# A chunked-attention and gated-FFN kernel whose order of work comes from another model of transfers and of two engines

## The chip, the cores and the metric

The kernel runs on one core of a Trainium2 chip. TensorE (PE) multiplies matrices, VectorE (DVE), ScalarE (ACT) and GpSimd (POOL) do elementwise work, and SyncE (SP) issues every transfer (DMA). Each engine runs its own instructions strictly in the order in which they stand in the program, and waits on semaphores for the others. The metric is the device time of one execution in microseconds (us), less being better. Three runs of the kernel before took 854.36, 854.88 and 857.61 us; the median is 854.88 us.

## What is computed

Inputs are float32: q, k, v of 8 batches x 8 heads x 576 positions x 64, w_in (512 x 2048) and w_out (2048 x 512).

```python
q_c, k_c, v_c = [a.reshape(B, H, 9, 64, D) for a in (q, k, v)]      # chunks of 64
scores = np.matmul(q_c, k_c.transpose(0, 1, 2, 4, 3)) / np.sqrt(D)
attn = np.exp(scores - scores.max(-1, keepdims=True))
attn = attn / (attn.sum(-1, keepdims=True) + 1e-09)
x = np.matmul(attn, v_c).reshape(B, H, S, D).transpose(0, 2, 1, 3).reshape(B * S, H * D)
h = x @ w_in                                                        # 4608 x 2048
g = h * (1.0 / (1.0 + np.exp(-1.702 * h)))
out = (g @ w_out).astype(np.float32)                                # 4608 x 512
```

## The kernel before

**Tiling.** The 4608 tokens are 36 tiles u of 128 and 9 blocks n of 512 (NB = 9, BT = 512); d_ff is 16 tiles j of 128 (NF = 16). A pair number g = 16 n + j names one block and one tile of d_ff. A float32 product is made of three matmuls: each operand is split into a high and a low part (`h`, `l`), and `w_h x_l + w_h x_h + w_l x_h` is summed in PSUM.

**Stages.** Blocks 0 and 1 use the plain product: steps h0_g and h_g, 12 matmuls of 128x512 (L1205 to L1207). Block 2 (g = 32 to 47) uses seven products instead of eight on halves, the scheme of Strassen and Winograd: for each pair p of tiles j there are seven products P1 to P7 of six matmuls of 128x256, in four phases ph0 to ph3 (`plan_seven`, L684 to L686). Blocks 3 to 8 go two at a time, s = 0, 1, 2, with the same seven products of six matmuls of 128x512 (`plan_two`, L770 to L772). After every product GELU and the split of g follow (steps gh_g on ACT, gl_g on DVE: L817, L721, L1232), and the second matmul, four steps o_g_0 to o_g_3 of three matmuls each (L1242 to L1244), into four PSUM banks po0 to po3 that hold a block's output until ob_n_t copies it (ACT for even t, DVE for odd) and st_n_t stores it. The copies go through two buffers, `ob`.

**Weights of the seven products.** `plan_prep` makes, for each p, sums of w_in's quarters on POOL (`sums`), splits them (phi on ACT, plo on DVE, L588), and writes all seven to a DRAM tensor `seven`: the three quarters that are no sums by out_a (steps pout0 to pout2, L595), the sums by out_s (pouts, L600). Block 2 loads them by phase (ld0 to ld3, L674, into a ring of six slots, 512 floats a product), blocks 3 to 8 by product (L763, six pieces).

**x's sums.** The seven products need sums of x as well. `plan_x(r, h, ..)` makes four differences t1 to t4 of 128x512 (L511, on POOL) for r = 0 (block 2) and, for each run of two blocks r = 1, 2, 3, for two halves h; ACT takes the high parts (L524) and DVE the low parts (L527).

**Attention** runs beside this, two tiles at a time (u = 4, 6, .. 34). From u = 6 on, q and k arrive as many small transfers (qk_i_n_u, L924 or L913, into one buffer `raw`), are transposed on DVE (tq0_u, tq1_u, L967), and step s_u on PE makes the scores of u (L983) and, in the same step, x of the pair before (L1057), which needs the transposed exponentials et_(u-2) of DVE (L1032), the load v1_(u-2) and both PSUM buffers `hp`. Between the two stand max and difference (mx, m), exp, sum (z) and POOL's normalisation n_u (L1013). v has one buffer, which s_(u+2) gives back.

**What sets the order.** `Plan` is a list scheduler that runs while the program is built. Every step is added with an engine, a cost in us written by hand, a rank, the events that it needs, and the buffers that it takes and gives. `emit` plays this list on model engines: whenever an engine is free, it takes the ready step of lowest rank. The order that comes out is the program's order on each engine; nothing of it is decided on the chip. ORDER fixes the first steps by name. In this model a small transfer keeps the DMA engine for its cost and lands 2.9 us later; a large one (`bulk`) issues in 0.5 us and then keeps a bus (BUS) for its cost. POOL and DVE know nothing of each other.

In the lists of order below a row is one instruction or several equal ones; the name ahead of `<-` is what is written, its last number only counts allocations.

Of the kernel before, what the change touches and what calls it, by code (L numbers as in the profile page):

```python
# [9 lines left out]
F32 = mybir.dt.float32  # L10
# [4 lines left out]
AF = mybir.ActivationFunctionType  # L15
ALU = mybir.AluOpType
AX = mybir.AxisListType

PE, ACT, DVE, POOL, DMA, BUS = "pe", "act", "dve", "pool", "dma", "bus"
# [28 lines left out]
class Plan:  # L48
# [6 lines left out]
    HANDOVER = {None: 0.0, PE: 0.25, ACT: 0.12, DVE: 0.12, POOL: 0.15, DMA: 2.9, BUS: 2.4}  # L55
    TABLE_LOAD = 1.3

    def __init__(self, buffers):
        self.free = dict(buffers)
        self.steps = []  # L60
        self.first = {}

    def add(self, engine, cost, rank, fn, need=(), make=None, take=(), give=(), table=None):
        self.steps.append((engine, cost, rank, fn, tuple(need), make, tuple(take), tuple(give), table))

    def bulk(self, cost, rank, fn, need=(), make=None, take=(), give=()):

        self.add(DMA, 0.5, rank, fn, need=need, make=make + "~", take=take)
        self.add(BUS, cost, rank, None, need=[make + "~"], make=make, give=give)

    def emit(self):
# [12 lines left out]
        busy = {e: 0.0 for e in self.HANDOVER}  # L84
        first = {e: names.split()[::-1] for e, names in self.first.items()}
# [3 lines left out]
        while left:  # L89
            for e, heap in ready.items():  # L90
                while heap and busy[e] <= now + 1e-9:
# [13 lines left out]
                    _, cost, _, fn, _, make, take, give, tab = self.steps[pick]  # L105
# [7 lines left out]
                    left -= 1  # L113
                    busy[e] = now + cost
                    post(now + cost, 0, () if e in (DMA, BUS) else give)
                    post(now + cost + self.HANDOVER[e], 0, give if e in (DMA, BUS) else ())
                    post(now + cost, 1, (make, e, True))
                    post(now + cost + self.HANDOVER[e], 1, (make, e, False))
            assert at or not left, sorted((s[2], s[5]) for h in ready.values() for s in [self.steps[i] for _, i in h])[:9]
            now = at[0][0] if at else now  # L120
            while at and at[0][0] <= now + 1e-9:
# [4 lines left out]
                else:  # L126
                    ev, engine, same = what
                    for i in users.get(ev, ()):
                        to = self.steps[i][0]
                        if (to == BUS or (to == engine and engine != DMA)) != same:  # L130
                            continue
# [10 lines left out]
def tile_chunk_attention_ffn(  # L142
# [29 lines left out]
    RANKS = (2.5, 8.5, 14.0, 16.5, 26.5, 29.5, 34.5, 39.0, 46.0, 53.5, 59.0, 72.0, 73.5, 78.5, 84.5, 101.5)  # L172
    K_ACT = (1, 2, 3, 4)
    LEAD = 12
# [31 lines left out]
    X_SLOT = (9, 10, 11, 12, 6, 4, 2, 3, 15, 5, 13, 14, 7, 8)  # L206
# [19 lines left out]
    def plan_w(j):  # L226
# [48 lines left out]
        plan.add(DMA, 2.85, rank - 5.5, load, need=need, make=e("raw"), take=[f"w{j}"])  # L275
# [1099 lines left out]
```

## Time and profile before

| what | value |
| --- | --- |
| median of three runs | 854.88 us |
| the profiled execution, its own time | 857.12 us |
| its span, first to last instruction | 855.3 us |
| granted TensorE clock, mean | 0.991 |
| PE busy | 821.2 us, 96% of the span |
| DVE / ACT / POOL busy | 550.1 / 378.0 / 125.2 us |
| DMA packets, bytes | 235303, 128.95 MB |

A busy PE is the bound, so what counts is where PE stood idle and at which clock it ran. A row of the view of waits reads: engine, what it was about to write, its line, then what ended the wait, and us in total, times, longest. A row of a timeline reads: start, length, engine, line, what is written from what, how many, and in brackets the idle time before it with what ended it. A row of the view by stretches reads: the stretch, its length, busy us of PE, PE's weight load, DVE, ACT, POOL (with counts), the granted clock of PE, the share in which the DMA engines were busy, and GB/s.

### The profile page before, as it was taken

What the parts mean: (1) busy time and instruction counts of PE and PEld (TensorE: products, weight loads), DVE (VectorE), ACT (ScalarE), POOL (GpSimd) and SP (SyncE); (2) the same over time, 40 slices, a digit from 0 to 9 for tenths busy, and PEclk for the clock granted to TensorE, in tenths of its full rate; (3) what the DMA queues carried; (4) which work ended last, traced back from release to release, by engine and by line L of the source; (5) the groups of instructions that cost most, each with busy time, mean ns of one, the idle gap of its engine ahead of it and who ended that gap; (6) DMA issues with size and microseconds to landing.
All of it is one profiled execution on the core that took longest, in us unless ns stands there. A gap on an engine that the chain in (4) does not pass through costs nothing.

```text
span 855.3 us, 15198 instructions
## 1 busy us (share of the span) xinstructions
PE 821.2 (96%) x5894; PEld 680.0 (80%) x5894; DVE 550.1 (64%) x741; ACT 378.0 (44%) x557; POOL 125.2 (15%) x102
## 2 busy tenths in 40 slices
PE   7999997999998999999999999999999999999998
PEld 6888876888887887888887778888877788888786
DVE  5778966656965789757768877593468443443322
ACT  5989724526615246343436344342444222323222
POOL 1000343474100113000002310000022000000000
PEclk9999998999998999999999999999999999999999
DMA  9996765676469876765576446644441054444101
GB/s 231 326 310 185 205 185 161 173 221 182 90 212 248 222 186 140 192 160 136 146 176 163 74 102 154 164 132 118 133 124 38 1 154 120 122 123 124 49 1 50
DMA packets 235303, 128.95 MB, mean 151 GB/s; under 512 B 186592, under 2 KB 200928, under 8 KB 235232
## 3 DMA queue, kind: packets, MB, share of 16 engines
q1 hardware_dynamic: 235232, 127.98, 56.3%
q8 instruction: 47, 0.77, 0.4%
q14 instruction: 24, 0.20, 0.1%
HBM read 103.81 MB, written 24.12 MB: 150 GB/s over the span
## 4 chain that ended last, share of the span: by engine, by line
PE 68%; SPq 10%; DVE 9%; DMA 8%; ACT 3%; issue 2%; POOL 1%; DVEq 0%; POOLq 0%; ACTq 0%
PE po L1242 11%; PE po L1243 11%; PE po L1244 11%; PE hp L770 8%; PE hp L772 8%; PE hp L771 8%; SPq L924 5%; DMA raw<-in_moe_w_out_dram 3%; PE x L1057 2%; DMA w<-seven 2%; PE s L983 2%; DVE w L527 1%; DVE g_l L817 1%; DVE eT L1032 1%; PE hp L1205 1%
## 5 line engine op out<-in xcount | busy, mean ns | idle before, releaser
L1242 PE MATMUL po<-w,g_l 128*128 128x512 f32 x576 | 228.8, 397 | 8.3 <-DVE g_l L817 5.9
L1243 PE MATMUL po<-w,g_h 128*128 128x512 f32 x576 | 225.1, 391 | 0.0
L1244 PE MATMUL po<-w,g_h 128*128 128x512 f32 x576 | 224.7, 390 | 0.0
L1242 PEld LDWEIGHTS po<-w,g_l 128*128 128x128 f32 x576 | 108.5, 188 | 35.8 <-DVE g_l L817 10.0
L1244 PEld LDWEIGHTS po<-w,g_h 128*128 128x128 f32 x576 | 108.4, 188 | 23.0
L1243 PEld LDWEIGHTS po<-w,g_h 128*128 128x128 f32 x576 | 108.6, 189 | 20.9
L808 ACT ACTIVATE g<-g 128x512 f32<-128x512 f32 x48 | 30.2, 632 | 143.1 <-DVE g L759 142.9
L770 PE MATMUL hp<-w,w 128*128 128x512 f32 x224 | 87.5, 391 | 2.2 <-DVE w L527 1.6
L772 PE MATMUL hp<-w,w 128*128 128x512 f32 x224 | 87.2, 389 | 0.0
L771 PE MATMUL hp<-w,w 128*128 128x512 f32 x224 | 87.2, 389 | 0.0
L1032 DVE STREAM_TRANSPOSE eT<-e 32x512 f32<-32x512 f32 x120 | 84.2, 702 | 1.9
L1013 POOL TENSOR_TENSOR e<-e,r 128x1024 f32<-128x1024 f32 x16 | 32.3, 2017 | 326.0 <-DVE r L1010 240.0
L817 DVE TENSOR_TENSOR g_l<-g,g_h 128x512 fp32r<-128x512 f32 x48 | 39.5, 822 | 53.9 <-ACT g_h L813 53.7
L813 ACT ACTIVATE g_h<-g 128x512 fp32r<-128x512 f32 x48 | 30.3, 630 | 74.5 <-PE po L1244 72.5
L967 DVE STREAM_TRANSPOSE qkT<-raw 128x1024 f32<-128x1024 f32 x30 | 37.0, 1238 | 25.8 <-DMA raw<-in_k_dram 15.0
L1205 PE MATMUL hp<-x_l,w 128*128 128x512 f32 x120 | 48.1, 401 | 5.1 <-DVE g_l L1232 5.1
L770 PEld LDWEIGHTS hp<-w,w 128*128 128x128 f32 x224 | 42.0, 188 | 12.4 <-DVE w L527 1.5
L772 PEld LDWEIGHTS hp<-w,w 128*128 128x128 f32 x224 | 42.0, 188 | 8.7
L771 PEld LDWEIGHTS hp<-w,w 128*128 128x128 f32 x224 | 42.1, 188 | 8.6
L1207 PE MATMUL hp<-x_h,w 128*128 128x512 f32 x120 | 47.6, 396 | 1.3 <-DVE w L266 1.3
L1206 PE MATMUL hp<-x_h,w 128*128 128x512 f32 x120 | 47.7, 397 | 0.0
L759 DVE TENSOR_TENSOR g<-hp,g 128x512 f32<-128x512 f32 x24 | 16.6, 691 | 43.6 <-PE hp L772 43.3
(140 smaller groups left out, 1385.9 us busy)
## 6 DMA issues: line engine op xcount, KB each, us to landing
w<-seven SPq DMA_DIRECT2D x120, 256.0 KB, 2.8
pieces<-seven SPq DMA_DIRECT2D x56, 256.0 KB, 2.9
w<-seven SPq DMA_DIRECT2D x24, 512.0 KB, 4.5
raw<-in_moe_w_in_dram SPq DMA_DIRECT2D x16, 512.0 KB, 7.6
raw<-in_moe_w_out_dram SPq DMA_DIRECT2D x16, 512.0 KB, 7.9
out_dram<-ob SPq DMA_DIRECT2D x32, 256.0 KB, 2.2
seven<-w SPq DMA_DIRECT2D x16, 512.0 KB, 3.8
raw<-in_q_dram SPq DMA_DIRECT2D x208, 32.0 KB, 2.6
```

The costliest lines, as they stand in the source:

```text
L770: nc.tensor.matmul(hp, w[:, 0, c], xl[:, c], start=c == 0, stop=False)
L771: nc.tensor.matmul(hp, w[:, 0, c], xh[:, c], start=False, stop=False)
L772: nc.tensor.matmul(hp, w[:, 1, c], xh[:, c], start=False, stop=c == 1)
L817: nc.vector.tensor_tensor(gl, words(h, late), gh.bitcast(F32), op=ALU.subtract)
L924: nc.sync.dma_start(t[p0 : p0 + 32, i, n, o // 32 : (o + c) // 32, :], src[b, 2 * n + h, s : s + c, d * 32 : d * 32 + 32].rearrange("(t j) ...
L1032: nc.vector.transpose(st["et"][po : po + 32, :, 32 * a : 32 * a + 32], st["e"][pi : pi + 32, :, 32 * b : 32 * b + 32],)
L1205: nc.tensor.matmul(hp, wh, xl, start=cc == 0, stop=False)
L1206: nc.tensor.matmul(hp, wh, xh, start=False, stop=False)
L1207: nc.tensor.matmul(hp, wl, xh, start=False, stop=cc == NCC - 1)
L1242: nc.tensor.matmul(po, gl[:, c], w[:, 0, :], start=first, stop=False)
L1243: nc.tensor.matmul(po, gh[:, c], w[:, 0, :], start=False, stop=False)
L1244: nc.tensor.matmul(po, gh[:, c], w[:, 1, :], start=False, stop=last)
```

## The change

The model behind the order changes, and with it some work:

- Transfers. BUS is gone. A transfer has a count and a time each; each issues in 0.48 us, not before the transfer eight places ahead of it has landed (LANES = 8), lands no earlier than 2.1 us after its start, and not before the one ahead plus its own time.
- Port. Steps of POOL, and those of DVE marked `port`, are made to wait for each other in the model.
- x's sums of r = 1, 2, 3 are done by DVE (L535 of the changed kernel) instead of POOL: 24 instructions. Those of r = 0 stay on POOL.
- w_in's quarters go to DRAM in two transfers for each p (512 KB and 256 KB) instead of three of 256 KB, with rank `first + 3` instead of `first - 6`; P1 and P2 now lie interleaved in `seven`, and blocks 3 to 8 read them in runs of 1 KB. The sums' rank is `first - 3` instead of `first - 2`.
- Block 2's phases are P1 P2, P6 P7, P5 P3, P4 instead of P1, P2 P6, P5 P3, P7 P4, and their sums are built by seven DVE instructions of 128x256 and one ACT copy for each p, where five DVE instructions (three of 128x256, two of 128x512) and one ACT copy did it.
- LEAD, the ranks of the 16 pairs and some slots are other numbers.

```diff
-    HANDOVER = {None: 0.0, PE: 0.25, ACT: 0.12, DVE: 0.12, POOL: 0.15, DMA: 2.9, BUS: 2.4}
+    HANDOVER = {None: 0.0, PE: 0.25, ACT: 0.12, DVE: 0.12, POOL: 0.15, DMA: 0.1}
+    ISSUE, LANES, LANDING = 0.48, 8, 2.1
...
     def bulk(self, cost, rank, fn, need=(), make=None, take=(), give=()):
-        self.add(DMA, 0.5, rank, fn, need=need, make=make + "~", take=take)
-        self.add(BUS, cost, rank, None, need=[make + "~"], make=make, give=give)
+        self.add(DMA, (1, cost), rank, fn, need=need, make=make, take=take, give=give)
+    def transfers(self, now, count, each):
+        for _ in range(count):
+            start = max(now, self.landed[-self.LANES])
+            now = start + self.ISSUE
+            self.landed.append(max(start + self.LANDING, self.landed[-1] + each))
+        return now, self.landed[-1]
...
+                    if port:
+                        cost += max(0.0, held[POOL if e == DVE else DVE] - now)
+                        held[e] = now + cost
+                    if e == DMA:
+                        free, done = self.transfers(now, *cost)
+                        cost = free - now
+                    else:
+                        done = now + cost
...
-    RANKS = (2.5, 8.5, 14.0, 16.5, 26.5, 29.5, 34.5, 39.0, 46.0, 53.5, 59.0, 72.0, 73.5, 78.5, 84.5, 101.5)
+    RANKS = (-10.5, 9.0, 14.0, 21.0, 26.5, 28.5, 35.0, 39.0, 45.5, 49.5, 61.0, 72.0, 76.5, 85.5, 94.0, 101.5)
-    LEAD = 12
+    LEAD = 27
+    PREP = -3
+    SUMS = 3
+    ON_POOL = (0,)
...
+        T_ENGINE, T_COST, engine = (POOL, 1.05, nc.gpsimd) if r in ON_POOL else (DVE, 0.69, nc.vector)
...
-            nc.gpsimd.tensor_tensor(raw(out), raw(a), raw(b), op=ALU.subtract)
+            engine.tensor_tensor(raw(out), raw(a), raw(b), op=ALU.subtract)
...
-            plan.bulk(0.75, first - 6, lambda i=i: out_a(i), need=[w0 if i < 2 else w1], make=outs[i])
+        for i in range(2):
+            plan.bulk((1.5, 0.85)[i], first - PREP, lambda i=i: out_a(i), need=[(w0, w1)[i]], make=outs[i])
...
-    PHASE = (("P1",), ("P2", "P6"), ("P5", "P3"), ("P7", "P4"))
-    LOADS = ((0, 1), (1, 3), (3, 5), (5, 7))
+    PHASE = (("P1", "P2"), ("P6", "P7"), ("P5", "P3"), ("P4",))
+    LOADS = ((0, 2), (2, 4), (4, 6), (6, 7))
...
-            nc.scalar.activation(st["d"][:, 2:3], st[0][:, :1], AF.Copy)
+            nc.scalar.activation(st["d"][:, 1], st[0][:, 0], AF.Copy)
+        def drain_0b():
+            d = st["d"]
+            add(d[:, 0], st[0][:, 1], d[:, 1])
         def drain_1():
             d = st["d"]
-            add(d[:, 0:2], st[1], bc(d[:, 2:3]))
+            add(d[:, 1], st[1][:, 0], d[:, 1])
+            add(d[:, 2], st[1][:, 1], d[:, 1])
         def drain_2():
             d = st["d"]
-            add(d[:, 2:3], st[2][:, :1], d[:, 1:2])
-            add(d[:, 3:4], st[2][:, 1:], d[:, 2:3])
+            st["f"] = f = more.tile([P, 2, 256], F32, tag="wtmp", name=f"f_{g0}")
+            add(d[:, 3], st[2][:, 0], d[:, 1])
+            add(f[:, 1], st[2][:, 0], d[:, 2])
+            add(d[:, 3], st[2][:, 1], d[:, 3])
         def drain_3():
-            st["f"] = f = more.tile([P, 2, 256], F32, tag="wtmp", name=f"f_{g0}")
-            add(f, bc(st[3][:, :1]), st["d"][:, 1:3])
-            add(f[:, :1], st[3][:, 1:], f[:, :1])
+            add(st["f"][:, 0], st[3][:, 0], st["d"][:, 2])
...
-        plan.add(ACT, 0.42, g0 - 6, drain_0, need=[e("ph0")], make=e("d0"), take=["tmp"], give=["hp"])
+        plan.add(ACT, 0.42, g0 - 6, drain_0, need=[e("ph0")], make=e("d0"), take=["tmp"])
+        plan.add(DVE, 0.42, g0 - 6, drain_0b, need=[e("d0")], make=e("d0b"), give=["hp"])
```

What the new order does to three places, engine by engine.

SP between the loads of pair 8 (`raw_8`) and the first output stores (`ob_0`), before:

```order
L924 DMA raw_8_1103<-in_k_dram 32x8x32 x16
L595 DMA seven_80<-w_8_828 128x2x256 x2
L595 DMA seven_80<-w_9_872 128x2x256
L595 DMA seven_80<-w_10_960 128x2x256 x2
L595 DMA seven_80<-w_11_976 128x2x256
L595 DMA seven_80<-w_12_1064 128x2x256 x2
L595 DMA seven_80<-w_13_1101 128x2x256
L924 DMA raw_10_1322<-in_q_dram 32x8x32 x4
L595 DMA seven_80<-w_14_1173 128x2x256 x2
L595 DMA seven_80<-w_15_1218 128x2x256
L924 DMA raw_10_1322<-in_q_dram 32x8x32 x8
L315 DMA v_8_1455<-in_v_dram 128x8x64
```

The same place in the changed kernel:

```order
L964 DMA raw_8_1069<-in_k_dram 32x8x32 x16
L620 DMA seven_80<-w_12_1028 128x1024
L623 DMA seven_80<-w_13_1118 128x2x256
L620 DMA seven_80<-w_14_1172 128x1024
L623 DMA seven_80<-w_15_1190 128x2x256
L964 DMA raw_10_1339<-in_q_dram 32x8x32 x8
L338 DMA v_8_1442<-in_v_dram 128x8x64
L964 DMA raw_10_1339<-in_q_dram 32x8x32 x4
L1298 DMA out_0_dram<-ob_0_0_1452 128x512
```

The first store of block 0's output (the last row above) is in the order before the row behind those shown; 25 transfers stand between pair 8's last load and it before, 17 now. The stores of w_in's quarters that are gone from here stand further up, the first of them (`w_0`) ahead of 28 loads of pair 6.

DVE in block 2, around the transposes of pair 16 (`qkT_16`) and of pair 14's exponentials (`eT_14`), before:

```order
L721 TENSOR_TENSOR g_l_34_2676<-d_34_2582,g_h_34_2675 128x512
L1032 STREAM_TRANSPOSE eT_14_2605<-e_14_2481 32x16x32 x2
L721 TENSOR_TENSOR g_l_35_2710<-f_34_2683,g_h_35_2709 128x512
L689 TENSOR_TENSOR d_36_2728<-hp_36_1_2715,d_36_2728 128x512
L527 TENSOR_TENSOR w_12_1064<-xs_12_2479,w_11_976 128x2x256
L967 STREAM_TRANSPOSE qkT_16_2506<-raw_16_2223 128x1024
L689 TENSOR_TENSOR d_36_2728<-hp_36_2_2749,d_36_2728 128x256 x2
```

The same place in the changed kernel:

```order
L719 TENSOR_TENSOR f_34_2676<-hp_34_3_2664,d_34_2626 128x256
L1007 STREAM_TRANSPOSE qkT_16_2551<-raw_16_2182 128x1024
L1072 STREAM_TRANSPOSE eT_14_2712<-e_14_2561 32x16x32 x2
L756 TENSOR_TENSOR g_l_34_2692<-d_34_2626,g_h_34_2691 128x512
L1072 STREAM_TRANSPOSE eT_14_2712<-e_14_2561 32x16x32 x6
L756 TENSOR_TENSOR g_l_35_2734<-f_34_2676,g_h_35_2733 128x512
L719 TENSOR_TENSOR d_36_2741<-hp_36_0_2699,d_36_2741 128x256
```

The second transpose of pair 16 now stands ahead of g_l_34 and g_l_35 instead of behind them, and on PE step s_16 stands after o_35_1 instead of after o_36_1, ahead of eight steps that it followed (o_35_2, o_35_3, ph2_36, ph3_36, ph0_38, ph1_38, o_36_0, o_36_1). On SP the load v1_14 that s_16 needs stands 339th instead of 357th among all transfers, and the last load of pair 16 333rd instead of 344th.

DVE at the end of run s = 0, where x's sums of r = 2 are due (`xt_2_0`, `xs_24`), before (POOL holds the four sums):

```order
L991 TENSOR_REDUCE m_26_4949<-s_26_4863 128x16
L1253 COPY ob_3_1_4964<-po_3_1_3795 128x512
L527 TENSOR_TENSOR w_3_540<-xs_24_4942,w_2_524 128x2x256
L527 TENSOR_TENSOR w_5_636<-xt_2_0_4956,w_15_1218 128x2x256
L817 TENSOR_TENSOR g_l_79_4979<-g_0_7_4804,g_h_79_4978 128x512
L527 TENSOR_TENSOR w_4_583<-xs_24_4942,w_6_729 128x2x256
```

The same place in the changed kernel:

```order
L1031 TENSOR_REDUCE m_26_4957<-s_26_4871 128x16
L1293 COPY ob_3_1_4970<-po_3_1_3811 128x512
L535 TENSOR_TENSOR xt_2_0_4975<-xs_24_4950 128x512
L535 TENSOR_TENSOR xs_24_4950<-xs_24_4950,xs_20_4001 128x512
L857 TENSOR_TENSOR g_l_79_4984<-g_0_7_4816,g_h_79_4983 128x512
L535 TENSOR_TENSOR xt_2_0_4975<-xs_24_4950 128x512
L535 TENSOR_TENSOR xs_20_4001<-xs_20_4001,xt_2_0_4975 128x512
```

Two of the sums stand where two low parts stood, and the low parts follow behind g_l_79.

117 lines of the change are left out of this document (64 added, 53 removed).

## The prediction

> **What bounds the kernel now.** I read the page's busy times first, then the view by stretches, then TensorE's waits, then the timelines around each wait.
>
> ```profile
> PE 821.2 (96%) x5894; PEld 680.0 (80%) x5894; DVE 550.1 (64%) x741; ACT 378.0 (44%) x557; POOL 125.2 (15%) x102
> ```
>
> TensorE is busy for 821.2 of 855.3 us, and the change neither adds nor removes a matmul: the same seven products run in another grouping. So the time can fall only by TensorE's 34 us of idle time and by whatever it lost to a lower clock.
>
> ```profile
> 220.00:340.00 120.00, 110.51 (x1095) 97.06 (x1095) 92.37 (x134) 52.60 (x82) 18.57 (x12) 0.97 0.72 190
> 340.00:460.00 120.00, 120.00 (x885) 99.31 (x884) 83.21 (x118) 48.11 (x75) 6.80 (x5) 1.00 0.65 164
> ```
>
> By stretches the idle time is lumpy: 9.5 us in block 2 (220 to 340), none from 340 to 460, although VectorE is busy there for 83 of 120 us.
>
> ```profile
> PE po L1242 <- DVE g_l L817: 5.9, 6, 1.4
> PE hp L1205 <- DVE g_l L1232: 5.1, 2, 4.9
> PE x L1057 <- DMA v<-in_v_dram: 3.7, 1, 3.7
> PE x L419 <- ACT first_b L410: 2.4, 2, 1.3
> PE hp L684 <- issue: 1.8, 1, 1.8
> PE hp L770 <- DVE w L527: 1.6, 2, 1.1
> PE warm L1314 <- POOL ident masks.py:199: 1.4, 1, 1.4
> PE hp L1207 <- DVE w L266: 1.3, 1, 1.3
> PE po L1242 <- DVE g_l L721: 1.3, 1, 1.3
> PE po L1242 <- DVE ob L1253: 1.0, 2, 0.6
> PE s L983 <- DVE qkT L967: 0.9, 1, 0.9
> ```
>
> Leaving out the two of the start (L419, warm), whose steps ORDER still fixes, these are 22.6 us, 17 waits. They are what the new order can win. Some cost more than their length:
>
> ```profile
> 135.80:138.40 2.60, 2.58 (x6) 2.10 (x7) 2.53 (x4) 0.00 (x0) 0.00 (x0) 0.50 1.06 298
> 138.40:142.00 3.60, 3.60 (x12) 2.80 (x12) 3.60 (x5) 0.58 (x1) 1.92 (x2) 0.68 0.44 71
> ...
> 256.30:260.20 3.90, 3.90 (x19) 3.77 (x20) 2.29 (x4) 2.60 (x5) 0.00 (x0) 0.56 1.03 332
> ...
> 267.00:270.80 3.80, 3.80 (x40) 3.16 (x41) 0.69 (x1) 2.65 (x5) 0.00 (x0) 0.55 0.98 256
> ```
>
> After the waits of 4.9, 1.8 and 3.7 us the granted clock was near half. The loss is (1 - 0.50) x 2.60 + (1 - 0.68) x 3.60 = 2.5 us, (1 - 0.56) x 3.90 = 1.7 and (1 - 0.55) x 3.80 = 1.7: 5.9 us together.
>
> The Trainium skill's page "TensorE: Matmul & The Clock Gate", section "Part 1: The HAM clock gate", has the clock halve only after an idle window of about 3.4 us. By that rule the wait of 1.8 us would have cost no clock and the gain below would be 1.7 us less; the row for 256.30 shows 0.56, so the trace decides and I keep the 1.7. So 22.6 + 5.9 = 28.5 us is all that the order can bring.
>
> **The change, part by part.**
>
> *(a) The weights' split moves ahead of the exponentials' transposes.* The wait of 1.3 us (L1207) comes here:
>
> ```profile
> 106.57 2.14 DVE L1032 STREAM_TRANSPOSE eT<-e 32x512 f32<-32x512 f32 x3
> ```
>
> The last low part of w stood behind eight such transposes (2.14 / 3 = 0.7 us each, 5.6 us), and now stands ahead of them; the wait goes. Against that, a 512 KB store is put ahead of 28 loads of pair 6, and those were already late:
>
> ```profile
> 88.89 1.25 DVE L967 STREAM_TRANSPOSE qkT<-raw 128x1024 f32<-128x1024 f32 x1 [1.18 <-DMA raw<-in_k_dram]
> ```
>
> At the 332 GB/s of the crowded stretch above, 512 KB take 1.6 us. TensorE takes up the scores of pair 6 as soon as this transpose ends, so between 0 and 1.6 us are lost; I take 1.0. Net gain 0.3.
>
> *(b) Fewer stores ahead of the output's.* The longest wait, 4.9 us, is a chain that ends in SP's queue:
>
> ```profile
> 122.47 2.15 SPq L595 DMA_DIRECT2D seven<-w  x3
> 124.65 5.26 SPq L924 DMA_DIRECT2D raw<-in_q_dram  x8
> 130.02 0.40 SPq L315 DMA_DIRECT2D v<-in_v_dram  x1
> 130.51 1.00 SPq L1258 DMA_DIRECT2D out_dram<-ob  x2
> 133.81 1.35 DVE L1253 COPY ob<-po 128x512 f32<-128x512 f32 x2 [8.22 <-DMA out_dram<-ob]
> ```
>
> VectorE sat 8.2 us before copying po1 until the first store had landed and given back an `ob` buffer; the g_l behind that copy holds the PSUM buffer that TensorE wants. The store was issued at 130.51 because 25 transfers stood ahead of it. Eight of them are gone. The rows from 122.47 on hold 12 transfers in the 8.0 us up to the store, 0.67 each: with eight fewer the store issues 5.4 us earlier, at about 125. That covers the 4.9 us with little to spare; I leave 0.5. The clock's 2.5 us goes with the wait. Gain 4.9 + 2.5 - 0.5 = 6.9. Were SP's pace then held up by the larger stores, 2 us of it would stay.
>
> *(c) Block 2: loads, v and the place of s_16.* Waits of 3.7 (v1_14), 1.8 and 0.9 us with 3.4 us of clock, 9.8 together.
>
> ```profile
> 205.59 3.98 SPq L913 DMA_DIRECT2D raw<-in_q_dram  x8
> ...
> 248.69 3.96 SPq L913 DMA_DIRECT2D raw<-in_k_dram  x8
> ```
>
> ```profile
> 254.17 1.25 DVE L967 STREAM_TRANSPOSE qkT<-raw 128x1024 f32<-128x1024 f32 x1 [6.46 <-DMA raw<-in_k_dram]
> ```
>
> ```profile
> 219.46 0.28 PE L684 MATMUL hp<-xe,w 128*128 128x256 f32 x1
> ...
> 245.92 0.40 PE L1242 MATMUL po<-w,g_l 128*128 128x512 f32 x1
> ```
>
> From 205.59 to 252.65 SP issues the 78 transfers up to pair 16's last, 0.60 each; without anything in between eight take 3.98, 0.50 each. VectorE then waits 6.5 us in front of the transpose. In the new order 77 transfers stand in this run, the eleven large ones spread out (four stood together), and v1_14 stands 18 places further up, so the 3.7 us goes. But s_16 moves ahead of eight steps and its transpose ahead of g_l_34 and g_l_35, and both then wait behind it on VectorE. I take a pace of 0.56, 43 us; the run's start, which hangs on the transpose of pair 14, 11 us earlier (9 transfers fewer at 0.6 ahead of it, and about 6 us by which TensorE is ahead after a and b): 194.5. Last issue 237.6, landing 2.4 later, the transpose 1.25: 241.3; two transposes of 0.7 and g_l_34 at 0.7 behind it: 243.4. TensorE went from the first product of the block at 219.46 to o_34_0 at 245.92; 6 us earlier, it reaches o_34_0 at about 239.9. It waits 3.5 us. Then six more transposes stand ahead of g_l_35, 4.2 us and its own 0.7 against 2.7 us of matmuls: 2.2 more. So 5.7 come back in place of 9.8. Gain 4.1; at a pace of 0.50 it is all of 9.8, at 0.60 it is 1.0 and, with a wait long enough to lower the clock, -1.5.
>
> The phases' sums cost VectorE 7 x 0.42 instead of 3 x 0.42 + 2 x 0.68 for each p, 0.3 us more, 2.6 in eight p:
>
> ```profile
> L689 DVE TENSOR_TENSOR d<-hp,d 128x256 f32<-128x256 f32 x16 | 6.8, 422 | 4.3 <-PE hp L686 3.7
> ```
>
> VectorE has 28 us free in the 120 of this stretch; matmuls of the o steps cover it. Without that cover it costs 2.6.
>
> *(d) x's sums by VectorE.* The waits on g_l L817 but the last (4.5 us), on w L527 (1.6), on g_l L721 (1.3) and on ob (1.0) all lie where POOL makes these sums: 8.4 us.
>
> ```profile
> 458.69 1.62 POOL L511 TENSOR_TENSOR xs<-xs,xs 128x512 f32<-128x512 f32 x1
> ```
>
> ```profile
> 459.31 1.55 DVE L527 TENSOR_TENSOR w<-xt,w 128x512 fp32r<-128x512 f32 x1 [0.15 <-ACT w L524]
> 460.78 1.77 DVE L817 TENSOR_TENSOR g_l<-g,g_h 128x512 fp32r<-128x512 f32 x1
> ...
> 464.17 0.68 DVE L527 TENSOR_TENSOR w<-xt,w 128x512 fp32r<-128x512 f32 x1
> ```
>
> While POOL adds, the same VectorE instruction takes 1.55 or 1.77 instead of 0.68. A sum on VectorE should be like that last row, 0.68: 24 x 0.68 = 16.3 us of VectorE in place of some 35 us of POOL at 1.3 to 1.6 each. Where TensorE waited for g_l_79, two sums (1.4 us) now stand in front of it, where a low part at 0.82 and one at 1.55 stood, and it runs 1.1 us faster: about 2 us earlier against a wait of 0.8. I count 7.0 of the 8.4 us. If the sums only take the place of the waits, it is 0, and at worst all 16.3 us would show; the stretch from 340 on, where 83 us of VectorE in 120 made no wait, is the nearest row and speaks for the first.
>
> *(e) The end.* At 809 the step o_143_0 waited 1.4 us; o_142_2 and o_142_3, 1.4 us of matmuls, now stand ahead of it. Gain 1.3.
>
> *(f) Rows not worked through.* Some hundred rows move that I did not follow, ranked by costs that are not the trace's. TensorE's waits of this kernel are near 1 us each; I allow 3.5 of them, 3.5 us, between 0 and 17, the count of the old ones. The loads in runs of 1 KB fall in the stretch from 340 on, with six pieces in flight and no wait of TensorE: nothing.
>
> Sum: 0.3 + 6.9 + 4.1 + 7.0 + 1.3 - 3.5 = 16.1 us. The profiled execution took 857.1 us (855.3 of span, 1.8 around it), so it would take 841.0; it lies 2.2 us above the median of the runs, 854.9, which gives **839 us**.
>
> **The rivals.**
>
> *All old waits go and none comes:* 854.9 - 28.5 = 826. For it: most old waits have a visible cause that is gone. Against it: (c).
>
> *VectorE takes POOL's place:* the sums hold g_l as long as POOL's lock did, (d) and (e) bring nothing: 839 + 8.3 = 847. For it: g_l and the low parts queue on one engine with 16 us more work. Against it: the 1.77 us rows go.
>
> *Pair 16 is later than I think:* the pace stays 0.60; 77 x 0.04 = 3.1 us more wait, and the wait of then 7 us lowers the clock, 1.7 to 2.5: 839 + 5.2 = 844.
>
> *The order only moves the waits,* the model's costs being no better than before: 855.
>
> *Slower: the PSUM buffers of block 2.* There are two `hp`. Before, ph0's was free after ACT's copy alone; now it holds two products and needs ACT's copy and then VectorE's d0b, which queues behind whatever VectorE runs, in-order: a transpose at 0.7 to 1.25 us, or one that waits for a load, as the 6.5 us row. Sixteen pairs of phases at 1.5 us each cost 24 us: 839 + 24 = 863. It decides from 1 us a pair on. For it: VectorE is busy 92 of 120 us there. Against it: the o steps between the pairs, four of 0.68 us, cover 2.7 us.
>
> **How the numbers follow.** Forecast 839 (its own range 831 to 845): 0.45. All gone, 826: 0.06. VectorE, 847: 0.15. Pair 16, 844: 0.14. Waits moved, 855: 0.10. Slower, 863: 0.10. A measurement here tells about 0.5%, 4.3 us, from no change. Faster is then the first four, 0.80; same 0.10; slower 0.10. The range 827 to 853 leaves out the last two cases and about half of the 826 one, and a little of the others' edges: 0.2.
>
> **What would show it.** (b): no idle time before L1205's successor near 130 us, clock 1.00 throughout 120 to 142. (c): the wait of L1057 on v gone; in its place waits of o (L1282) on g_l in block 2 near 240, behind a transpose that waits for raw; if there are none, (c) was too low. (d): low parts and g_l at 0.6 to 0.8 us throughout, 24 sums on VectorE near 0.68, POOL down by some 35 us, and no g_l wait beyond 0.5 us at the three ends of runs. (e): nothing over 0.3 us after 700. The forecast is wrong if TensorE's idle time past the start stays above 18 us, or if block 2's products wait on d0b sixteen times.

## The result

The changed kernel took 844.36 us in the median of four runs (843.36 to 846.79), against 855.5 us for the kernel before in the same comparison (854.36 to 857.61). The ratio is 0.9871, with a 95% interval of 0.9842 to 0.9900: 1.3% or 11 us faster, where 839 us had been forecast. The profiled execution took 844.18 us with a span of 842.4 us.

### The profile page after: what moved, and what is told of

Same layout as the page of the kernel before. It is cut to its first block, busy times and chain, and to the rows that moved or that the text cites. A ratio compares the mean times of both kernels' runs of the same rounds, so it can differ in the third digit from the quotient of the medians.

```text
span 842.4 us, 15212 instructions
## 1 busy us (share of the span) xinstructions
PE 818.4 (97%) x5894; PEld 680.0 (81%) x5894; DVE 549.1 (65%) x781; ACT 378.4 (45%) x557; POOL 86.7 (10%) x78
## 4 chain that ended last, share of the span: by engine, by line
PE 81%; SPq 9%; DMA 4%; DVE 3%; issue 1%; ACT 1%; POOL 0%; DVEq 0%; ACTq 0%; POOLq 0%
PE po L1282 14%; PE po L1283 13%; PE po L1284 13%; PE hp L810 9%; PE hp L811 9%; PE hp L812 9%; SPq L964 3%; SPq L338 2%; PE hp L1245 2%; PE hp L1246 2%; PE hp L1247 2%; DMA w<-seven 2%; PE s L1023 2%; PE x L1097 1%; SPq L258 1%
## 5 line engine op out<-in xcount | busy, mean ns | idle before, releaser
L857 DVE TENSOR_TENSOR g_l<-g,g_h 128x512 fp32r<-128x512 f32 x48 | 35.2, 737 | 44.5 <-ACT g_h L853 44.2
L1007 DVE STREAM_TRANSPOSE qkT<-raw 128x1024 f32<-128x1024 f32 x30 | 37.2, 1241 | 27.8 <-DMA raw<-in_k_dram 15.7
L1245 PE MATMUL hp<-x_l,w 128*128 128x512 f32 x120 | 47.8, 398 | 5.8 <-DVE g_l L1272 5.8
L795 DVE TENSOR_TENSOR d<-hp,d 128x512 f32<-128x512 f32 x48 | 32.9, 684 | 19.0 <-PE hp L812 18.7
```

The costliest lines, as they stand in the source:

```text
L857: nc.vector.tensor_tensor(gl, words(h, late), gh.bitcast(F32), op=ALU.subtract)
L1007: nc.vector.transpose(st["tr"][:, i].rearrange("p n (t j) -> p (n t) j", j=32), st["raw"][:, i].rearrange("p n t j -> p (n t) j"),)
L1245: nc.tensor.matmul(hp, wh, xl, start=cc == 0, stop=False)
```

## The profile after

The page's busy times:

```profile
PE 818.4 (97%) x5894; PEld 680.0 (81%) x5894; DVE 549.1 (65%) x781; ACT 378.4 (45%) x557; POOL 86.7 (10%) x78
```

TensorE is busy 2.8 us less with the same instructions; the time lost to a lower clock, worked out below, fell by 2.7 us. Its idle time fell from 34.1 to 24.0 us. The view of TensorE's waits:

```profile
PE hp L1245 <- DVE g_l L1272: 5.8, 3, 3.3
PE po L1282 <- ACT ob L1291: 4.8, 1, 4.8
...
PE po L1282 <- DVE g_l L756: 1.3, 3, 0.5
...
PE hp L715 <- DVE d L719: 0.5, 1, 0.5
```

The waits at the ends of the runs (on g_l L817, w L527 and a copy to ob) and the wait on v are gone. In their place stand three on a g_l of block 1 (L1272) and one of 4.8 us on `ob`, which the kernel before did not have. By stretches, two of the rows on which the table rests:

```profile
220.00:340.00 120.00, 113.41 (x1109) 99.62 (x1108) 97.41 (x164) 54.21 (x83) 7.62 (x4) 0.97 0.74 199
...
460.00:520.00 60.00, 60.00 (x384) 49.39 (x383) 50.45 (x72) 28.03 (x41) 4.07 (x2) 1.00 0.47 105
```

| TensorE idle in | before | after |
| --- | --- | --- |
| 0 to 120 us | 7.5 | 7.0 |
| 120 to 220 | 5.1 | 5.8 |
| 220 to 340 | 9.5 | 6.6 |
| 340 to 460 | 0.0 | 0.7 |
| 460 to 680 | 6.6 | 0.2 |
| 680 to the end | 5.3 | 3.9 |

From 340 us on nearly all the idle time has gone. What is left past the start lies mostly between 130 and 305 us, and two waits there still cost clock:

```profile
129.80:133.20 3.40, 0.31 (x2) 0.00 (x0) 1.78 (x3) 3.33 (x5) 0.00 (x0) 1.00 1.01 240
133.20:138.00 4.80, 4.55 (x13) 3.59 (x14) 3.98 (x7) 1.37 (x3) 0.86 (x1) 0.64 0.63 161
236.00:241.00 5.00, 0.17 (x2) 0.08 (x1) 1.29 (x2) 0.72 (x2) 0.00 (x0) 0.93 0.81 214
241.00:244.00 3.00, 3.00 (x8) 2.42 (x9) 2.79 (x6) 2.95 (x4) 0.00 (x0) 0.50 0.56 151
```

That is (1 - 0.64) x 4.8 = 1.7 us and (1 - 0.50) x 3.0 = 1.5 us, 3.2 together, where it was 5.9.

The wait at 130 is the one that term (b) was to remove. SP's own queue before:

```profile
111.62 1.93 SPq L924 DMA_DIRECT2D raw<-in_k_dram  x4
113.65 6.19 SPq L595 DMA_DIRECT2D seven<-w  x9
```

SP's queue in the changed kernel, and then VectorE:

```profile
111.58 4.39 SPq L964 DMA_DIRECT2D raw<-in_k_dram  x9
...
117.92 0.61 SPq L623 DMA_DIRECT2D seven<-w  x1
118.79 5.69 SPq L964 DMA_DIRECT2D raw<-in_q_dram  x8
124.58 0.40 SPq L338 DMA_DIRECT2D v<-in_v_dram  x1
125.02 3.56 SPq L964 DMA_DIRECT2D raw<-in_q_dram  x4
128.67 0.87 SPq L1298 DMA_DIRECT2D out_dram<-ob  x2
...
149.67 4.59 SPq L964 DMA_DIRECT2D raw<-in_q_dram  x8
...
176.18 0.82 SPq L964 DMA_DIRECT2D raw<-in_q_dram  x2
...
201.85 1.28 SPq L953 DMA_DIRECT2D raw<-in_q_dram  x3
```

```profile
117.52 1.25 DVE L1007 STREAM_TRANSPOSE qkT<-raw 128x1024 f32<-128x1024 f32 x1 [3.31 <-DMA raw<-in_k_dram]
...
130.97 0.69 DVE L1293 COPY ob<-po 128x512 f32<-128x512 f32 x1 [6.15 <-DMA out_dram<-ob]
...
148.40 1.24 DVE L1007 STREAM_TRANSPOSE qkT<-raw 128x1024 f32<-128x1024 f32 x1
...
174.90 1.25 DVE L1007 STREAM_TRANSPOSE qkT<-raw 128x1024 f32<-128x1024 f32 x1 [3.23 <-DMA raw<-in_k_dram]
...
200.58 1.25 DVE L1007 STREAM_TRANSPOSE qkT<-raw 128x1024 f32<-128x1024 f32 x1 [5.32 <-DMA raw<-in_k_dram]
```

The store issues at 128.67, 1.8 us earlier than before (130.51), not 5.4. Eight transfers are gone from ahead of it, but two things kept it back. SP is through with pair 8's last k load at 115.97 (111.58 + 4.39), 2.4 us later than before (111.62 + 1.93 = 113.55): twelve stores stand ahead of it as before, but half of them are now of 512 KB. And the first q load of pair 10 cannot issue before the k transpose of pair 8 has read the one buffer `raw`: it issues at 118.79, the transpose ends at 117.52 + 1.25 = 118.77. The four stores that are left in front of that load end at 118.53, so this second thing alone cost 0.26 us here, but taking out those four as well would have brought the load no further up.

It is the same in the later pairs: 148.40 + 1.24 and 149.67, 174.90 + 1.25 and 176.18, 200.58 + 1.25 and 201.85. There SP stood still for 0.8, 2.2 and 1.9 us in front of the load. So there is a loop: k transpose of a pair, 32 or 64 small loads of the next pair on SP (with what stands between them), that pair's k transpose. I call one round a turn. Not every turn is closed by its loads: the last k load of pair 10 had landed at 142.7, and VectorE came to the transpose at 148.40 straight from other work. Which engine TensorE then waits for is a matter of what stands behind such a transpose or load in an in-order queue.

## The experiments

All are the changed kernel with one edit or with several edits together, except the second, which is the kernel before with one edit. A diff shows the lines on which an edit turns. Times are medians; ratios are to the kernel before on the same chip, with their 95% intervals. The changed kernel itself stands at 0.9871.

### Who makes x's sums

Undone in the changed kernel (e1), with the order of every other instruction kept:

```diff
-            engine.tensor_tensor(raw(out), raw(a), raw(b), op=ALU.subtract)
+            nc.gpsimd.tensor_tensor(raw(out), raw(a), raw(b), op=ALU.subtract)
```

> The changed kernel with one thing undone: x's sums of r = 1, 2, 3 (24 instructions) run on GpSimd again, in the place of the order where VectorE ran them. Theory of the prediction, (d): GpSimd's sums slow VectorE's low parts and g_l from 0.68 to some 1.7 us, and TensorE's waits on g_l L857, w L551 and ob at the ends of the runs come back, 5 to 8 us: 849 to 852 us. Rival: it was the order that took these waits away, not the engine: VectorE's instructions are as slow as in the kernel before, but no wait over 0.5 us comes back: 843 to 846 us.

Measured: 845.01 us, 0.9873 (0.9854 to 0.9892), the same as the changed kernel. VectorE's timeline of this kernel, at the end of run s = 0:

```profile
456.33 1.46 DVE L857 TENSOR_TENSOR g_l<-g,g_h 128x512 fp32r<-128x512 f32 x1 [2.02 <-ACT g_h L853]
457.72 1.78 DVE L551 TENSOR_TENSOR w<-xt,w 128x512 fp32r<-128x512 f32 x1
459.42 0.68 DVE L1293 COPY ob<-po 128x512 f32<-128x512 f32 x1
```

VectorE's instructions are as slow beside GpSimd as in the kernel before (1.46 and 1.78 us in place of 0.68), but TensorE's idle time from 460 to 520 and from 630 to 680 us is 0.1 and 1.1 us, not 2.9 and 3.6. The rival holds, but for one wait of 1.0 us on a g_l at 658, where it allowed 0.5: in the new order most of the slow instructions have slack.

Up to 287 us this kernel runs the same instructions in the same order as the changed one, so the two profiles also show how far two executions differ: the first product of block 2 starts at 216.55 here and at 218.93 there, the wait on `ob` is 5.7 and 4.8 us, and a turn differs by up to 0.7 us.

Done alone in the kernel before (e2):

```diff
-            nc.gpsimd.tensor_tensor(raw(out), raw(a), raw(b), op=ALU.subtract)
+            (nc.vector if r else nc.gpsimd).tensor_tensor(raw(out), raw(a), raw(b), op=ALU.subtract)
```

> The kernel before with one thing changed: the 24 sums run on VectorE, in the place of the order where GpSimd ran them. Theory of the prediction, (d): the 8.4 us of waits at the ends of the runs nearly go, 5 to 8 us: 847 to 850 us. Rival: in an order that was not planned for it the sums hold up g_l on VectorE (16 us more work there) and the waits stay or grow: 854 to 858 us.

Measured: 849.04 us, 0.9924 (0.9905 to 0.9943), 6.5 us less than before; idle 1.4 us in each of the two stretches. The theory holds here, inside its 847 to 850. Of the prediction's 8.4 us of waits 4.7 are gone in the profile. Some of the gain lies elsewhere: the wait of 1.8 us at 256 is gone too, although the first sum that moved stands at 292. The two results together: the engine and the order are two cures of the same waits. Either alone removes more than half of them, and with the new order in place the engine adds nothing that can be measured.

The Trainium skill's page "SBUF — State Buffer", section "🔬 SBUF: two separate sides", says that GpSimd and VectorE's instructions with two SBUF inputs take a shared port pair in turns, for a whole instruction each. The rows above (1.46 and 1.78 us beside GpSimd) agree; e1 shows that such a lock need not cost time.

### The stores that TensorE waited for

The first two output stores moved up on SP's queue (e3; each step is put behind the one beside it):

```diff
+    MOVE = (("v0_8", "st_0_2"), ("qk_0_2_10", "v0_8"))
```

> The changed kernel with SP's order altered in one place: the load v0_8 and the four loads qk_0_2_10 go behind the first two output stores (st_0_0, st_0_2), which so stand five transfers further up. Theory A: the wait of 3.3 us at 130 is SP's queue alone, the store issues at 124.6 instead of 128.7, the wait and the clock's loss behind it go (3.3 + 1.7 us), and later waits stay as they are: 839 to 840 us. Rival B: the waits at 182, 202 and 236 hang on SP's queue too, which does not run earlier because TensorE does; they grow by what TensorE is ahead, and the time is given back: 843 to 845 us. Rival C: VectorE's copy waits for something else than the store: the wait stays where it is.

Measured: 846.18 us, 0.9881 (0.9861 to 0.9901). The wait at 130 fell from 3.3 to 0.7 us with its loss of clock, and the waits of L1245 in all only from 5.8 to 4.8: there are now 1.2 us at 137 and 2.9 at 181, and 2.8 us at 267, all behind a transpose on VectorE. Rival B: given back. The median is 1.8 us above the changed kernel's, inside the spread of its own six runs (843.38 to 847.22).

Block 1's stores moved up (e4):

```diff
+    MOVE = (("ld3_34", "st_1_1"), ("ld0_36", "ld3_34"), ("qk_1_2_16", "ld0_36"))
```

> The changed kernel with SP's order altered in another place: ld3_34, ld0_36 and the eight loads qk_1_2_16 go behind the stores st_1_0 and st_1_1 of block 1, which so stand ten transfers further up. Theory A: the wait of 4.8 us at 236 and the clock's loss behind it (1.5 us) go, and in their place come the waits that the prediction named in (c), of o_34_0 and o_35_0 behind the transposes of pair 16 and of pair 14's exponentials, about 2 us each: 840 to 842 us. Rival B: nothing takes their place: 837 to 839 us. Rival C: the wait only moves to the next instruction that needs a late transfer and is as long: 843 to 845 us.

Measured: 845.73 us, 0.9882 (0.9857 to 0.9906). The wait on `ob` is gone, and TensorE and VectorE show what took its place:

```profile
247.76 0.80 PE L1282 MATMUL po<-w,g_l 128*128 128x512 f32 x1 [5.05 <-DVE g_l L756]
```

```profile
244.44 1.25 DVE L1007 STREAM_TRANSPOSE qkT<-raw 128x1024 f32<-128x1024 f32 x1 [5.70 <-DMA w<-seven]
245.61 1.37 DVE L1072 STREAM_TRANSPOSE eT<-e 32x512 f32<-32x512 f32 x2
247.02 0.69 DVE L756 TENSOR_TENSOR g_l<-d,g_h 128x512 fp32r<-128x512 f32 x1
```

It is o_34_0 behind the k transpose of pair 16, as the prediction's (c) named it, 5.05 us long. (The bracket of the transpose names a load of weights; pair 16's last k load landed at 244.06, 0.4 us ahead of the transpose.) Rival C holds: the wait has moved and is as long, and the time is at the edge of that rival's 843 to 845. In the changed kernel it was hidden behind the wait on `ob`.

### What sets a turn

The weights' 32 stores on GpSimd's queue (e5; out_a likewise):

```diff
-            nc.sync.dma_start(seven[p, :, at : at + 1024], w)
+            nc.gpsimd.dma_start(seven[p, :, at : at + 1024], w)
```

> The changed kernel, with the 32 stores of the seven products' weights (out_a and out_s) issued by GpSimd's queue instead of SP's, each at the same place of the program. Theory A: from 80 to 270 us SP's queue is the bound, by the count of its transfers at 0.5 to 0.6 us each; 32 fewer take 16 us off it, and the waits at 130, 182, 202 and 236 (3.3 + 1.1 + 1.7 + 4.8 us) go with the clock's loss behind them (3 us): 830 to 834 us. Rival B: the bytes bind, not the issues (DMA share 0.63 to 0.95 there); who issues makes no difference: 843 to 846 us. Rival C: issuing on GpSimd takes VectorE's or GpSimd's time: over 847 us.

Each store of 512 KB of a quarter as two of 256 KB, 8 more transfers on SP (e6):

```diff
-                nc.sync.dma_start(seven[p, :, :1024], w.rearrange("p a b -> p (a b)"))
+                [nc.sync.dma_start(seven[p, :, 512 * c : 512 * c + 512], w[:, c]) for c in range(2)]
```

> The changed kernel, with each 512 KB store of a quarter of w_in issued as two of 256 KB (8 more transfers on SP ahead of the first output store, the same bytes; the count of the kernel before). Theory A, SP's queue is the bound by its count: the first output store issues about 4 us later, and the wait at 130 grows from 3.3 to about 7 us or the later ones do: 847 to 849 us. Rival B, the bytes bind: 843 to 846 us.

The output stores on GpSimd's queue (e7):

```diff
-                nc.sync.dma_start(out[b * S + s : b * S + s + c, :], ob[o : o + c])
+                nc.gpsimd.dma_start(out[b * S + s : b * S + s + c, :], ob[o : o + c])
```

> The changed kernel, with the output stores (32 steps of o_store) issued by GpSimd's queue, so that none stands behind SP's loads. Theory A: the waits at 130 and 236 go (3.3 + 4.8 us and 3.2 us of clock), but pair 16's loads, only 6 transfers nearer on SP's queue (3 us), hold o_34_0 as they did when only block 1's stores were moved up, by 2 to 6 us: 838 to 842 us. Rival B: the stores were all of it: 833 to 835 us. Rival C: nothing is won: 843 to 846 us.

The edits of e5 and e7 together (e8):

> Both of the two kernels beside it: all stores on GpSimd's queue, all loads on SP's. Theory A: nothing in blocks 0 to 2 waits for a transfer any more; TensorE's waits past the start fall under 4 us and the clock stays at 1.00: 827 to 832 us. Rival B, the bytes bind: 840 to 846 us. Rival C, GpSimd's own queue holds the output stores behind the weights' stores and its sums: 836 to 842 us.

Measured: e5 846.03 us, 0.9887 (0.9869 to 0.9906); e6 846.77 us, 0.9900 (0.9887 to 0.9912); e7 844.38 us, 0.9875 (0.9860 to 0.9890); e8 851.09 us, 0.9928 (0.9905 to 0.9950). None of the gains came. The theory that these had in common, that SP's queue binds by the count of its transfers wherever they stand, falls; e6 lies at the edge of that theory's 847 to 849, but by its time only. Its queue, between pair 8's loads and the first output store:

```profile
117.32 0.87 SPq L620 DMA_DIRECT2D seven<-w  x2
...
120.12 0.61 SPq L623 DMA_DIRECT2D seven<-w  x1
120.83 5.02 SPq L964 DMA_DIRECT2D raw<-in_q_dram  x8
...
127.39 2.06 SPq L964 DMA_DIRECT2D raw<-in_q_dram  x4
129.55 0.87 SPq L1298 DMA_DIRECT2D out_dram<-ob  x2
```

The store issues at 129.55, 0.9 us later for eight more transfers, not 4. Behind six stores of 256 KB the 12 q loads take 5.02 + 2.06 = 7.1 us; behind the changed kernel's four stores of the same bytes they took 5.69 + 3.56 = 9.3. What the fewer stores saved, the loads behind them lost. That speaks for the bytes, rival B of e5 and e6, at this place.

In e7 the waits on `ob` at 130 and 236 are gone, but 1.2 us stay at 131, and 2.1 and 2.0 us stand at 246 and 251, 2.3 at 181 and 2.1 at 265 in their place, again behind transposes. In e5 the waits past 120 us fell, but 2.4 us came at 89 to 95, where VectorE had waited 3.2 us for the q loads of pair 6; the stores no longer wait their turn on SP there, which may be why. And with all of these stores off SP the first q load of pair 10 issues at 118.83 and the first output store at 128.75, no earlier than in the changed kernel: the load has to wait for the k transpose. e8 is slower than the changed kernel, and than any of its three forecasts: a transpose of pair 12 waited 8.0 us and TensorE 5.6 us behind it.

What the runs did share led to the loop as a theory. From the k transpose of pair 8 to that of pair 18 (their starts in VectorE's timeline) it took:

| kernel | pair 8 | pair 18 | us between | TensorE busy in them |
| --- | --- | --- | --- | --- |
| before | 115.5 | 290.7 | 175.2 | 163.8 |
| e2 | 114.3 | 286.7 | 172.4 | 161.8 |
| changed | 117.5 | 283.6 | 166.0 | 154.1 |
| e1 | 116.5 | 282.1 | 165.6 | 153.8 |
| e3, e4 | 117.0, 116.0 | 284.7, 281.8 | 167.7, 165.8 | 154.3, 153.2 |
| e5, e6 | 117.6, 118.9 | 281.3, 285.0 | 163.7, 166.1 | 154.7, 152.1 |
| e7, e8 | 117.8, 117.5 | 280.0, 285.6 | 162.2, 168.1 | 150.2, 155.8 |
| e9, e10 | 117.9, 116.8 | 281.9, 280.4 | 164.0, 163.6 | 151.1, 150.8 |
| e11 | 128.5 | 300.5 | 172.1 | 152.5 |
| e12 | 116.2 | 278.5 | 162.3 | 154.2 |

The periods are alike, but the last column offers a plainer reason than the loop: TensorE's own work between the two transposes is 150 to 164 us long. Only what is left, 8 to 14 us (20 in e11), and what a lower clock adds to the busy time can be any wait's doing. And between the kernel before and e2, which run the same instructions up to the first sum of r = 1, the period differs by 2.9 us. So the table alone does not show that the loop sets the pace; opening it is the test.

### The loop through one buffer

`raw` cut in two halves of the same size together, so that q's loads need not wait for the k transpose before (e9; the order of every engine is unchanged):

```diff
-            if i == n == 0:
-                st["raw"] = const.tile([P, 2, NP, 8, 32], F32, tag=raw_tag, name=f"raw_{u}")
-            t, src = st["raw"], (q, k)[i]
+            if n == 0:
+                st["raw", i] = const.tile([P, NP, 8, 32], F32, tag=raw_tag + str(i), name=f"raw_{u}_{i}")
+            t, src = st["raw", i], (q, k)[i]
```

> The changed kernel with the buffer raw cut in two halves, one for q and one for k (no more room than before, the order of every engine unchanged); the q loads of a pair then no longer wait until the k transpose of the pair before has read its half. Theory L (the loop): blocks 0 to 2 are bound by a loop through that one buffer, transpose of k, then the next pair's 32 or 64 small loads on SP, then the next transpose (25 to 27 us, 47 us for pair 16, in every kernel run so far); each turn gets shorter by the 1 to 2.5 us in which SP stood idle ahead of the first q load, the transposes from pair 12 on come 2 to 6 us earlier against the last one of pair 8, and the time falls by 3 to 6 us: 838 to 841 us. Rival: SP's issues themselves are the whole length of a turn, SP was never idle long enough: 843 to 846 us.

Measured: 841.65 us, 0.9837 (0.9816 to 0.9858). Four turns got 0.6 to 1.6 us shorter (pair 10 from 30.9 to 30.2, pair 12 from 26.5 to 24.9, pair 14 from 25.7 to 24.9, pair 16 from 47.3 to 45.8), pair 18's longer (35.7 to 38.2), and the time fell by 0.34% of the kernel before, 2.9 us. That is just short of the 3 to 6 us expected, its interval still overlaps the changed kernel's a little, and the turns of kernels that are equal up to there differ by as much: by up to 0.7 us between the changed kernel and e1, by up to 2.5 between the kernel before and e2. So opening the loop at q's half was worth some 3 us at best; k's half still ties k's loads to the k transpose, and it is not shown that the loop bounds blocks 0 to 2.

With the stores of e3 and e4 moved up as well (e10):

> The same two halves, and the output stores of blocks 0 and 1 moved up on SP's queue as in the two kernels with one store moved each. Theory L: the waits on the copies at 130 and 236 go, and what took their place at 180 and 246 (3.0 and 5.2 us, behind transposes that waited for raw) shrinks by what the loop gains, 2 to 5 us: 834 to 839 us. Rival: the place that is late next takes it all again: 843 to 846 us.

Measured: 841.77 us, 0.9840 (0.9818 to 0.9861). Nothing beside e9, between the two forecasts (834 to 839 and 843 to 846): the place that is late next took it, as the rival has it. The waits on `ob` became waits on g_l, 6.8 us in block 2 and 5.5 in block 1.

With two halves, and k's loads on GpSimd's queue (e11):

```diff
-                            nc.sync.dma_start(
+                            (nc.gpsimd if i else nc.sync).dma_start(
```

> The same two halves, and all loads of k in small pieces (16 or 32 for a pair) issued by GpSimd's queue, so that q and k are loaded side by side and SP has 16 to 32 issues fewer in a turn. Theory L: a turn falls from 25 to 27 us to under 18 us and from 47 to under 35 us, no transpose in blocks 0 to 2 waits for raw, and nearly all of the 11 us of waits past 120 us and the 3 us of clock go: 830 to 835 us. Rival B (bytes, or the landing, not the issues): 842 to 846 us. Rival C: the loads that wait on GpSimd's queue hold up its normalisation and sums, and that holds TensorE: over 846 us.

Measured: 868.49 us, 1.0174 (1.0147 to 1.0201), slower than the kernel before. The groups of GpSimd, its timeline and TensorE's waits:

```profile
L964 POOL DMA_DIRECT2D raw<-in_k_dram x208 | 121.6, 589 | 120.2 <-issue 97.7 <-DVE qkT L1007 13.4 <-DVE d L719 5.7
```

```profile
131.34 2.50 POOL L592 TENSOR_TENSOR whole<-w 128x512 f32<-128x512 f32 x2
133.79 1.75 POOL L964 DMA_DIRECT2D raw<-in_k_dram  x3
137.42 1.74 POOL L964 DMA_DIRECT2D raw<-in_k_dram  x3 [1.89 <-issue]
142.30 1.73 POOL L964 DMA_DIRECT2D raw<-in_k_dram  x3 [3.14 <-issue]
```

```profile
PE hp L1245 <- DVE g_l L1272: 15.2, 3, 11.3
PE s L1023 <- DVE qkT L1007: 10.9, 3, 6.4
```

Rival C, and more: the loads stand between GpSimd's sums, each takes 0.59 us of GpSimd, and in these rows it pauses 1.9 and 3.1 us between groups of three. The turn of pair 8 grew from 27.8 to 36.4 us. This run therefore doesn't test whether fewer issues on SP make a turn shorter.

Last, e10 with g_l put ahead of the late transposes on VectorE (e12):

```diff
+    MOVE = (..., ("tq0_10", "gl_17"), ("et0_10", "gl_24"), ("tq1_14", "gl_27"), ("tq1_16", "gl_34"),
+            ("et0_14", "tq1_16"), ("et2_14", "gl_35"), ("et_14", "et2_14"), ("tq0_18", "gl_37"))
```

> The kernel with two halves and the stores moved up, and VectorE's order altered in five places of blocks 1 and 2: g_l of pairs 17, 24, 27, 34 and 35, 36 and 37 stand ahead of a transpose that waited for raw or for GpSimd (tq0_10, et0_10, tq1_14, tq1_16 with et0_14, two of the exponentials' transposes, tq0_18) instead of behind it; all other orders are unchanged. Theory Q (the place in VectorE's queue): what holds TensorE is only that g_l stands behind a late transpose; 8 of the 13 us of waits past 120 us go and stay away: 832 to 835 us. Theory L (the loop): the transposes come no earlier for it; TensorE, ahead, then stands at the steps s_16 and s_18 and their x, which need the transposes themselves, and gives most of it back: 838 to 841 us. Rival: nothing changes, 841 to 843 us.

Measured: 839.23 us, 0.9821 (0.9795 to 0.9846), the lowest median of all, inside what theory L gave; its interval overlaps those of e9 and e10. VectorE's timeline, and TensorE's waits from 100 to 345 us:

```profile
242.40 1.25 DVE L1007 STREAM_TRANSPOSE qkT<-raw 128x1024 f32<-128x1024 f32 x1 [3.26 <-DMA w<-seven]
...
278.50 1.25 DVE L1007 STREAM_TRANSPOSE qkT<-raw 128x1024 f32<-128x1024 f32 x1 [2.28 <-DMA w<-seven]
```

```profile
PE po L1282 <- DVE g_l L756: 4.2, 3, 3.2
PE hp L1245 <- DVE g_l L1272: 1.5, 3, 0.9
PE hp L715 <- DVE g_l L1272: 1.4, 1, 1.4
PE s L1023 <- DVE qkT L1007: 1.1, 1, 1.1
...
PE po L1282 <- DVE g_l L1272: 0.7, 1, 0.7
```

Of the 5.5 us of waits on block 1's g_l in e10, 3.6 remain (1.5, 1.4 and 0.7), and TensorE now stands 1.1 us at a score step, on the transpose itself. The transposes came no earlier by it than by relieving SP: 162.3 us between pairs 8 and 18, as in e7. Moving one wait showed the next, as theory L said; but with TensorE busy for 154.2 of these us, the run does not tell the loop from TensorE's own work as what sets the pace of the pairs.

**What stays open** is what sets the length of a turn. In the changed kernel the turn of pair 14 holds 39 issues in 25.7 us; 32 follow the one before within 0.62 us, 15.7 us together, and six come later, 4.5 us beyond the usual pace. From pair 10 on, with 1 to 5 issues fewer in a turn, e5's were between 3.6 us shorter (pair 16) and 1.2 longer (pair 18), so the count of issues alone is not it. A kernel in which q and k come in fewer transfers would tell; it was not tried.

## Why the prediction was right, and where its size was not

The direction and the range held: 844.36 lies in 827 to 853, and in the likeliest case's own 831 to 845. It is 5 us above the 839. The mechanism held for (a), for the wait on v in (c) and for (e); (b) failed in the main, and (d) held for the waits and not for the engine alone. Each size below is from one profile before and one after. They add up to 11.4 us; the medians differ by 11.1.

| term | forecast | measured |
| --- | --- | --- |
| (a) split ahead of the transposes | 0.3 | 0.6 (idle to 120 us, 7.5 to 7.0) |
| (b) fewer stores ahead of the output's | 6.9 | 2.4 (wait 4.9 to 3.3, clock 2.5 to 1.7) |
| (c) block 2 | 4.1 | about 2 (9.8 to 6.1 of waits and 1.5 of clock) |
| (d) x's sums | 7.0 | about 8 (8.4 to 0.5) |
| (e) the end | 1.3 | 1.4 (5.3 to 3.9) |
| (f) rows not worked through | -3.5 | about -3 (0.9 and 1.6 at 182 and 202, 0.7 from 340 to 460) |

**(b) is the term that failed.** "12 transfers in the 8.0 us ... 0.67 each: with eight fewer the store issues 5.4 us earlier" took SP's queue as a row of transfers of equal length that closes up when some are taken out. The bytes stayed, in fewer and larger stores, and e6 shows what such a count is worth: eight transfers more, 0.9 us. The loads of pair 8 came 2.4 us later, and the q loads of pair 10 could not issue before the k transpose of pair 8 had freed `raw`, at 118.77; the store came 1.8 us earlier, and in e5, with the stores of the weights on another queue, no earlier than that. The prediction had a case for larger stores that hold up SP's pace, of 2 us, but did not take it into the sum. It left 0.5 of 4.9 us where 3.3 stayed. Its sign for (b), no idle time near 130 and a clock of 1.00, did not come; its sign of being wrong, over 18 us of idle time past the start, was not met either: from 120 us on there are 17.0.

**(c) had the place and not what stands in front of it.** The wait on v went, as forecast. The pace in pair 16's loads was 0.56 in the forecast, and is (243.22 - 201.85) / 77 = 0.54. But the run starts at 201.85, not 194.5. Of the 11 us about 6 were to be TensorE's lead, and there was none: the first product of block 2 starts 0.5 us earlier than before (219.46), since the waits at 182 and 202 had taken what (a) and (b) won.

```profile
218.93 0.28 PE L715 MATMUL hp<-xe,w 128*128 128x256 f32 x1
```

With that, block 1's stores, behind the same loads on SP, became late first and gave the 4.8 us on `ob`, a wait that the prediction did not have. e4 then brought out the wait that it did have, at o_34_0, with 5.05 us where 3.5 was forecast.

**(d) had the size and half of the cause.** The waits went and the sums take 0.69 us on VectorE, as forecast, but the prediction gave all of it to the engine. e1 shows that the new order would have removed most of them with GpSimd too (8.4 to 1.2 us); e2 that in the old order the engine alone removes 4.7 of the 8.4.

**(a), (e) and (f)** came out near their sizes. That (a)'s size is close says little, since the idle time to 120 us is 7.0 in the changed kernel and 5.7 in e1, which is the same there. (f) was an allowance, so that its size came out near is luck; the waits at 182 and 202 are of the kind that it allowed for: g_l behind a transpose.

**The rivals.** "DVE takes POOL's place" (847): there is no wait on g_l over 0.5 us at the ends of the runs. "Pair 16 is later" (844): the time is the measured one, by coincidence: its mechanism is not what happened, since the pace was faster than forecast. "The order only moves the waits" is what holds between 130 and 305 us, and only there. The slower rival, d0b and the two `hp`: one wait of 0.5 us in block 2, not sixteen of 1.5.

On the clock, the forecast of 5.9 us to be won by removing three waits was kept where the waits went; 3.2 us of it came back with the two that stayed or came.

## What to carry to other kernels

Before a queue is shortened, do not multiply the transfers taken out by a mean time: ask whether the bytes stay, and look for the transfer in the queue that waits for a buffer, since nothing behind that one moves up past it. When the time between equal instructions is the same in kernel after kernel, subtract what the busiest engine works in it before a loop is blamed, and then open the loop in one run. Two changes that cure the same wait should each be tried alone before either is called the reason.

## What the runs showed of the hardware

**The clock after a wait.** In the 14 profiles, of the waits of TensorE past 100 us, those of 1.3 to 1.9 us were followed by a full clock in 11 of 12 cases (the exception is the 1.83 us of the kernel before); those of 2.0 to 3.2 us by a lower clock in 8 of 17; those of 3.3 us and more in 17 of 18. Two waits and the 3.4 us behind each, of e7 (2.03 us, clock 0.59) and of e10 (3.57 us, clock 1.00):

```profile
250.73 0.50 PE L1282 MATMUL po<-w,g_l 128*128 128x512 f32 x1 [2.03 <-DVE g_l L756]
```

```profile
250.73:254.13 3.40, 3.40 (x45) 2.46 (x48) 1.13 (x3) 0.00 (x0) 0.00 (x0) 0.59 1.06 321
```

```profile
264.76 0.50 PE L1282 MATMUL po<-w,g_l 128*128 128x512 f32 x1 [3.57 <-DVE g_l L756]
```

```profile
264.76:268.16 3.40, 3.40 (x17) 2.86 (x18) 3.26 (x6) 0.00 (x0) 0.00 (x0) 1.00 0.98 252
```

So between 2 and 3.5 us the length of a wait alone does not decide whether it costs clock; what else does, these traces do not show. The Trainium skill's page "TensorE: Matmul & The Clock Gate", section "Part 1: The HAM clock gate", has a window of 3413 ns that runs freely, by which the place of a wait in time would count; that a whole idle window is needed is not what the 2.03 us row shows.

**Small loads behind larger stores.** Twelve loads of 32 KB took 9.3 us on SP behind four stores of 256 and 512 KB, and 7.1 us behind the same bytes in six stores of 256 KB (the changed kernel and e6, above).

**GpSimd as an issuer.** A small load issued by GpSimd takes 0.59 us of that engine, against about 0.5 us in SP's queue (eight in 3.98 us in the kernel before), and stands in line with its arithmetic (e11).
